# A fourth slot for copied products, the fifth tile's parts in unused quarters of weight tiles, and 2 KB of descriptor room for GpSimd's transfers

## The chip, the core and the metric

The kernel runs on one core of one Trainium2 chip. A time is the device time of one execution in microseconds (us); of several executions of one kernel the median counts. The engines are TensorE (PE; its weight loads PEld), VectorE (DVE), ScalarE (ACT), GpSimd (POOL) and SyncE (SP). Each runs its own list of instructions in order and waits on semaphores for the others. Transfers between HBM and the on-chip memory SBUF, or within SBUF, are issued by SP and POOL and moved by 16 DMA engines that both share. PE writes to PSUM only, in banks of 512 floats a partition.

## The reference

```python
attn_out = softmax(scale * rope(q) @ rope(k).T) @ v      # 2 x 8 heads, 576 rows, 64 columns
x = ((x @ w1) * (x @ w2)) @ w3 @ w_out                   # 1152 x 512, inner width 1024
# third part, on that x:
P = np.exp(logits - logits.max())                        # 1152 x 8, from x @ w_gate
for _ in range(8):
    P /= P.sum(1, keepdims=True) + 1e-09
    P /= P.sum(0, keepdims=True) + 1e-09
    P *= N / E
out = np.zeros((N, D), dtype=np.float32)
for e in range(E):                                       # E = 8 experts
    h = np.maximum(x @ w1[e], 0.0)                       # 512 -> 1024
    ye = h @ w2[e]                                       # 1024 -> 512
    out += P[:, e:e + 1] * ye
```

## The kernel before

The change lies in the third part, the eight experts. Each float32 operand is held as a high and a low part in the fast format, and a product is three matmuls (high by high, high by low, low by high). An expert is cut into two halves of its inner width, so there are 16 **steps** s. A step has two **groups** q = 2s and q = 2s+1 over the rows of x: the first takes 640 rows (columns of 320 on PE), the second 512 (columns of 256). In a group both matrix products, x @ w1 and h @ w2, are done by Strassen's scheme, on 2 x 2 blocks with seven block products in place of eight: A11, A12, A22, S1 to S4 in the code. `hidden(q, u, f)` (L823 to 835) is one product of the first kind, for half u of the inner width; `project(q, f)` (L939 to 961) is one of the second.

Since a PSUM bank must be free for the next product while several products are added into one result, three products of each kind are copied out by ACT: `hidden_copy` (L838) into `tmp`, and `project_copy` (L980) into `ztmp`, which has three slots. The three copies of a group are called zm1 (slot 0), zu2 (slot 1) and **zm7** (slot 2, from bank zQ). `project_sum` (L985, 987) adds a later product to a slot, `weight` (L1004) multiplies the slot by the rows' gate on ACT, and `added` (L1007) lets POOL add the slot to the result `acc` (the tile `sums` in the code) by an accumulating transfer of 256 KB. The three results are called c11, c21 and c22; c22 lies in slot 2. A slot is free for the next group's copy when its transfer has landed.

The 640 rows of a first group are five tiles of 128; Strassen's scheme covers four, and the **fifth tile** goes through plain products: `rest_hi` (L888) and `rest_lo` make high and low parts of it in a tile `HL` (hl in the rows), and `project_rest` (L968 to 970) multiplies them into bank zL, once a step.

Weights for Strassen's scheme need sums of blocks. SP loads blocks into `wide` and `sums` tiles; POOL adds others to them in place by accumulating transfers (`first_accumulate`, `second_accumulate`, all through L899): for each of the two halves of w1 a chain of three (256, 128, 128 KB; sadd in the code), and for w2 a chain of three (512, 256, 256 KB; tadd). `w1hi` (L1131) and `f2hi` (L933) are ACT's copies of the finished sums into high parts. So POOL issues 15 transfers a step: 6 of w1, 3 of w2 and 6 of `acc` (three a group), all in the order of its list.

The order on every engine comes from a planner: each task names its engine, a cost, a rank, what it needs and which slots it takes and frees; `Plan.order` plays that through and lets each engine take the ready task of least rank. POOL's transfers have a cost of KB/146 us on a made-up engine `sw`, with a signal of 1.5 us. The planner sets only the order. What is waited for on the chip is set by the real semaphores.

Of the kernel before, what the change touches and what calls it, by code (L numbers as in the profile page):

```python
# [11 lines left out]
F32 = mybir.dt.float32  # L12
F32R = mybir.dt.float32r
# [6 lines left out]
P = 128  # L20
# [33 lines left out]
class Plan:  # L54
# [2 lines left out]

    SIGNAL = dict(pe=0.28, act=0.14, dve=0.1, pool=0.12, sp=3.0, sw=1.5)  # L60
# [62 lines left out]
def attention_two_moes(ctx: ExitStack, tc: tile.TileContext, rope, qk, v, mw12, mw3t, mwo, wg, ew1, ew2, out):  # L123
# [10 lines left out]
    def f32(ap):  # L134
        return ap.bitcast(F32)
# [650 lines left out]
    pp = ctx.enter_context(tc.tile_pool(name="pp", bufs=1, space=PSUM))  # L786

    tmp = h_p.tile([P, 3, CN[0]], F32, name="tmp")
    ztmp = h_p.tile([P, 3, 2, 256], F32, name="ztmp")
    sums = h_p.tile([P, NTT, DM], F32, name="acc")  # L790
    lgT = sums[: 2 * E].rearrange("p t d -> p (t d)")[:, :NT]
    lg = h_p.tile([P, NTT, E], F32, name="lg")
# [46 lines left out]

    def hidden_sum(q, u, j, b, slot):  # L840
        n = CN[q % 2]
        dst, ps, was = raw[:, j, u, :n], bank[b, q, u][:, :n], tmp[:, slot, :n]
        if j == 0:
            dve.tensor_add(dst, ps, was)  # L844
        elif j == 1:
            dve.tensor_sub(dst, ps, was)
        else:
            negated(dst, ps, ALU.add, was)

    def rectified_last(q, u):  # L850
        n = CN[q % 2]
        act.activation(raw[:, 2, u, :n], bank["T", q, u][:, :n], AF.Relu)  # L852

    def source(f):
        if f in SLOT:
            return raw[:, SLOT[f], :, :256]
        return {S3: held, S4: held, S1: raw[:, 2, :, :256], S2: raw[:, 3, :, :256]}[f]

    def form_sum(f):

        a11, a12, a21, a22 = (raw[:, j, :, :256] for j in range(4))
        if f == S3:
            rectified(held, a11, ALU.subtract, a21)
        elif f == S1:
            rectified(a21, a22, ALU.subtract, a21)
        elif f == S2:
            rectified(a22, a22, ALU.add, held)
        else:
            rectified(held, a12, ALU.subtract, a22)
# [11 lines left out]
        else:  # L881
            dve.tensor_sub(HF[f][:, 1], source(f), f32(HF[f][:, 0]))

    rest = raw[:, :, :, 256 : CN[0]].rearrange("p (b i) u n -> p b (i u) n", b=2)
    restf = [HL[:, x].rearrange("p f (b n) -> p b f n", b=2) for x in range(2)]

    def rest_hi(b):
        act.activation(restf[0][:, b], rest[:, b], AF.Relu)  # L888

    def rest_lo(b):  # L890
        rectified(restf[1][:, b], rest[:, b], ALU.subtract, f32(restf[0][:, b]))

    def sums_tile(src):
        t = h_p.tile([P, 1024], F32, name="sums", bufs=3)
# [81 lines left out]
    def block(q, b, d):  # L976
        return sums[:, out_tiles(q, b), d * 256 : (d + 1) * 256]

    def project_copy(q, b, k):
        act.copy(ztmp[:, k], bank["z" + b, q])  # L980

    def project_sum(q, b, k, out=None):
        dst = ztmp[:, k] if out is None else block(q, *out)
        if b == "T":
            negated(dst, bank["zT", q], ALU.subtract, ztmp[:, k])  # L985
        else:
            dve.tensor_add(dst, bank["z" + b, q], ztmp[:, k])

    def weighted(q, b, d, t, src):
        tt = out_tiles(q, b).start + t  # L990
        acc, p = sums[:, tt, d * 256 : (d + 1) * 256], (npr if src is None else pr)[:, tt, q // 4 : q // 4 + 1]
        ps = bank["zT", q][:, t] if src is None else ztmp[:, src, t]
        dve.scalar_tensor_tensor(out=acc, in0=ps, scalar=p, in1=acc, op0=ALU.mult, op1=ALU.add)

    def weighted_part(q, b, d, t, src, negative):
        tt = out_tiles(q, b).start + t
        acc, p = sums[:, tt, d * 256 : (d + 1) * 256], (npr if negative else pr)[:, tt, q // 4 : q // 4 + 1]
        part = ztmp[:, src, t] if isinstance(src, int) else bank["z" + src, q][:, t]
        dve.scalar_tensor_tensor(out=acc, in0=part, scalar=p, in1=acc, op0=ALU.mult, op1=ALU.add)

    def weight(q, b, src):
        for t in range(2):
            tt = out_tiles(q, b).start + t
            act.activation(ztmp[:, src, t], ztmp[:, src, t], AF.Copy, scale=pr[:, tt, q // 4 : q // 4 + 1])  # L1004

    def added(q, b, d, src):
        pool.dma_start(block(q, b, d), ztmp[:, src], accum_op=ALU.add)  # L1007

    def weighted_rest(q):
        p = pr[:, 4, q // 4 : q // 4 + 1]  # L1010
# [93 lines left out]

# [51 lines left out]
    def hidden_tasks(q):  # L1156

        s, c = divmod(q, 2)
        n, was = CN[c], q - 1
        clear = {  # L1160
            0: [("hi", was, A11), ("lo", was, A11), ("sum", was, S3)],
            1: [("hi", was, A12), ("lo", was, A12), ("sum", was, S4)],
            2: [("hi", was, S1), ("lo", was, S1)],
            3: [("hi", was, S2), ("lo", was, S2), ("sum", was, S4)],
        }
        rests = lambda j: [] if c else old(*((("rest" + y, q - 2, j // 2)) for y in ("hi", "lo")))
        for u in range(2):
            r = 14 * q + 7 * u
            at = {f: r + k for k, f in enumerate(PRODUCTS)}
            h = lambda f: ("h", q, u, f)  # L1170
            a = lambda x: (x, q, u)
            more = {A11: [], S3: [], A12: [], S2: [a("m1")], A22: [a("m7")], S1: [a("u2")], S4: [("r", q, u, 3)]}
            for k, f in enumerate(PRODUCTS):
                weights = [("w1lo", s, u, int(f >= S1))] if s else []
                earlier = [h(PRODUCTS[k - 1])] if k else old(("h", q - 1 + u, 1 - u, S4))
                task(h(f), "pe", 6 * (0.1467, 0.12)[c], at[f], lambda u=u, f=f: hidden(q, u, f), weights + more[f] + earlier, [(HBANK[f], (q, u))] if f in OPENS else [])
            for k, (x, f, b) in enumerate((("m1", A11, "T"), ("u2", S2, "T"), ("m7", S3, "Q"))):
                task(a(x), "act", n - 30, at[f] + 0.2, lambda u=u, b=b, k=k: hidden_copy(q, u, b, k), [h(f)], [(x, (q, u))])
            for k, (j, f, b, y) in enumerate(((0, A12, "A", "m1"), (1, A22, "Q", "u2"), (3, S1, "T", "m7"))):
                needs = [h(f), a(y)] + old(*clear[j]) + rests(j)  # L1180
                task(("r", q, u, j), "dve", n, at[f] + 0.3, lambda u=u, j=j, b=b, k=k: hidden_sum(q, u, j, b, k), needs, (), [(y, (q, u))] + ([] if b == "T" else [(b, (q, u))]))
            needs = [h(S4)] + old(*clear[2]) + rests(2)
            task(("r", q, u, 2), "act", n, at[S4] + 0.3, lambda u=u: rectified_last(q, u), needs, (), [("T", (q, u))])

    def form_tasks(q):
# [19 lines left out]
        ):  # L1205
            task(("sum", q, f), "dve", 512, r + at - lead, lambda f=f: form_sum(f), needs)
        if c == 0:
            for b in range(2):
                task(("resthi", q, b), "act", 256, r + REST_AT - 5, lambda b=b: rest_hi(b), rows(2 * b, 2 * b + 1) + old(("zr", q - 2)))
                task(("restlo", q, b), "dve", 256, r + REST_AT - 5, lambda b=b: rest_lo(b), [("resthi", q, b)])  # L1210
            needs = [("restlo", q, b) for b in range(2)] + [("f2lo", s, ROW0), ("f2lo", s, ROW1)]
# [164 lines left out]
```

## Time and profile before

| | |
|---|---|
| median of 3 runs | 1167.8 us (1160.49 to 1169.78) |
| the profiled execution's own time | 1162.56 us |
| its span in the profile | 1160.8 us |
| mean granted clock of PE, share of full speed | 0.991 |
| PE busy | 1113.1 us (96%) |
| DVE, ACT, POOL busy | 795.2, 666.8, 325.2 us (69, 57, 28%) |
| transfers of POOL's queue | 55.33 MB, 32.2% of 16 engines' span |
| transfers of SP's queue | 109.94 MB, 30.0% |

Some 1.8 us of the execution lie outside the span. The experts' part fills the span from about 370 us to the end; attention and the first layer come before it. Matmuls are pipelined in the record: one of 256 columns is shown with 0.28 us and starts 0.12 us after the one before it, so a busy PE is read by the distance of starts. POOL is shown busy while it issues a transfer, not while the transfer runs.

### The profile page before, as it was taken

The numbers are of one execution on the slowest core, as the hardware profiler recorded it, in microseconds if no ns is written. First come the engines' busy times: TensorE is split into PE (matmuls) and PEld (weight loads), VectorE is DVE, ScalarE is ACT, GpSimd is POOL, SyncE is SP. The second block draws the span as 40 slices with busy tenths as digits, with TensorE's granted clock in tenths as the row PEclk, the third lists the DMA queues.
The fourth block names the chain that finished last, engine by engine and source line by source line (L and its number), as shares of the span: only waits on it lengthen the run. The fifth ranks groups of instructions, "written<-read, shape, count | busy, mean of one in ns | idle before, by whom it ended". The sixth has DMA issues, their size and how long they took to land.

```text
span 1160.8 us, 21261 instructions
## 1 busy us (share of the span) xinstructions
PE 1113.1 (96%) x8233; PEld 1054.2 (91%) x8233; DVE 795.2 (69%) x1391; ACT 666.8 (57%) x1391; POOL 325.2 (28%) x289
## 2 busy tenths in 40 slices
PE   9999999999999999999899999999999899899997
PEld 8887777999998899999899999999999899898997
DVE  7888675744333888767677776875777666586765
ACT  5877775643223556646566565655665546566553
POOL 1665521000000212323333333233333323333220
PEclk9999999999999999999999999999999999999999
DMA  7777733610004646777787887877868677687633
GB/s 237 235 223 205 240 110 110 218 55 1 1 1 121 145 103 164 144 154 162 143 182 149 168 173 140 183 140 165 177 147 167 128 151 161 137 182 142 139 55 103
DMA packets 86308, 167.20 MB, mean 144 GB/s; under 512 B 9536, under 2 KB 50240, under 8 KB 86208
## 3 DMA queue, kind: packets, MB, share of 16 engines
q0 software_dynamic: 47632, 55.33, 32.2%
q1 hardware_dynamic: 38032, 109.94, 30.0%
q8 instruction: 64, 1.05, 0.4%
q10 hardware_dynamic: 544, 0.59, 0.2%
q14 instruction: 36, 0.29, 0.1%
HBM read 112.02 MB, written 2.36 MB: 99 GB/s over the span
## 4 chain that ended last, share of the span: by engine, by line
PE 53%; DMA 10%; ACT 8%; issue 7%; DVE 3%; POOL 1%; ACTq 0%; DVEq 0%; POOLq 0%; SPq 0%
DMA acc<-ztmp 5%; PE T L833 4%; PE T L835 4%; PE T L834 4%; PE zT L959 3%; PE zT L961 3%; PE zT L960 3%; DMA sums<-sums 3%; PE s L153 3%; PE s L154 3%; PE s L155 3%; ACT hf L875 2%; PE Q L833 2%; PE zQ L961 2%; PE zQ L960 2%
## 5 line engine op out<-in xcount | busy, mean ns | idle before, releaser
L1007 POOL DMA_DIRECT2D acc<-ztmp x87 | 108.9, 1251 | 271.3 <-issue 63.6
L899 POOL DMA_DIRECT2D sums<-sums x92 | 94.0, 1024 | 213.0 <-issue 58.4
L959 PE MATMUL zT<-f,hf 128*128 128x256 f32 x496 | 141.0, 284 | 0.0
L961 PE MATMUL zT<-f,hf 128*128 128x256 f32 x496 | 140.4, 283 | 0.1
L960 PE MATMUL zT<-f,hf 128*128 128x256 f32 x496 | 140.4, 283 | 0.0
L899 POOL DMA_DIRECT2D sums<-in_ew_dram x46 | 54.6, 1187 | 216.8 <-DMA sums<-in_ew_dram 167.3
L833 PE MATMUL T<-x,w 128*128 128x320 f32 x256 | 84.0, 328 | 24.5 <-ACT tmp L838 22.0
L980 ACT COPY ztmp<-zQ 128x512 f32<-128x512 f32 x31 | 18.2, 586 | 146.0 <-DMA acc<-ztmp 131.5
L959 PEld LDWEIGHTS zT<-f,hf 128*128 128x128 f32 x496 | 95.1, 192 | 0.7 <-DVE acc L145 0.2
L961 PEld LDWEIGHTS zT<-f,hf 128*128 128x128 f32 x496 | 95.2, 192 | 0.3 <-DVE hf L148 0.3
L960 PEld LDWEIGHTS zT<-f,hf 128*128 128x128 f32 x496 | 95.1, 192 | 0.0
L148 DVE SCALAR_TENSOR_TENSOR y<-y 128x512 f32<-128x512 f32 x128 | 88.0, 688 | 2.4 <-ACT y L852 0.2
L844 DVE TENSOR_TENSOR y<-A,tmp 128x320 f32<-128x320 f32 (+1 forms) x64 | 29.0, 453 | 81.3 <-ACT tmp L838 66.2
L835 PE MATMUL T<-x,w 128*128 128x320 f32 x256 | 79.6, 311 | 0.0
L834 PE MATMUL T<-x,w 128*128 128x320 f32 x256 | 79.4, 310 | 0.0
L875 ACT ACTIVATE hf<-y 128x512 fp32r<-128x512 f32 x128 | 77.6, 629 | 2.9 <-DVE y L148 2.4
L1004 ACT ACTIVATE ztmp<-ztmp,pr 128x256 f32<-128x256 f32 x174 | 78.6, 500 | 0.7 <-DVE ztmp L145 0.3
L148 DVE SCALAR_TENSOR_TENSOR hf<-y,hf 128x512 fp32r<-128x512 f32 x96 | 64.8, 686 | 20.6 <-ACT hf L873 20.5
L153 PE MATMUL s<-x,w 128*128 128x320 f32 (+1 forms) x256 | 76.0, 297 | 0.3 <-DVE gf L678 0.3
L833 PEld LDWEIGHTS T<-x,w 128*128 128x128 f32 x256 | 48.6, 190 | 30.4 <-ACT tmp L838 24.5
L154 PE MATMUL s<-x,w 128*128 128x320 f32 (+1 forms) x256 | 75.8, 296 | 0.0
L155 PE MATMUL s<-x,w 128*128 128x320 f32 (+1 forms) x256 | 75.8, 296 | 0.0
(305 smaller groups left out, 3833.9 us busy)
## 6 DMA issues: line engine op xcount, KB each, us to landing
sums<-in_ew_dram SPq DMA_DIRECT2D x62, 512.0 KB, 4.0
acc<-ztmp POOLq DMA_DIRECT2D x87, 256.0 KB, 4.2
wide<-in_ew_dram SPq DMA_DIRECT2D x34, 512.0 KB, 4.8
wide<-in_ew_dram SPq DMA_DIRECT2D x30, 384.0 KB, 3.6
wide<-in_mw3t_dram SPq DMA_DIRECT2D x16, 512.0 KB, 5.0
wide<-in_mw_dram SPq DMA_DIRECT2D x16, 512.0 KB, 3.3
sums<-in_ew_dram POOLq DMA_DIRECT2D x16, 512.0 KB, 7.0
sums<-sums POOLq DMA_DIRECT2D x32, 256.0 KB, 3.8
```

The source lines that it names most:

```text
L148: dve.scalar_tensor_tensor(out=dst, in0=a, scalar=0.0, in1=b, op0=ALU.max, op1=op)
L153: pe.matmul(ps, wh, xh, start=(i == 0), stop=False)
L154: pe.matmul(ps, wh, xl, start=False, stop=False)
L155: pe.matmul(ps, wl, xh, start=False, stop=(i == n - 1))
L833: pe.matmul(ps, h[:, ws], x[0], start=(first and k == 0), stop=False, **kw)
L834: pe.matmul(ps, h[:, ws], x[1], start=False, stop=False, **kw)
L835: pe.matmul(ps, l[:, ws], x[0], start=False, stop=(k == 1), **kw)
L899: pool.dma_start(dst, src, accum_op=ALU.add)
L959: pe.matmul(ps[:, t], h, wh[:, u], start=(opens and u == 0), stop=False, **kw)
L960: pe.matmul(ps[:, t], h, wl[:, u], start=False, stop=False, **kw)
L961: pe.matmul(ps[:, t], l, wh[:, u], start=False, stop=(u == 1), **kw)
L1007: pool.dma_start(block(q, b, d), ztmp[:, src], accum_op=ALU.add)
```

## The change

Five edits. `ztmp` gets a fourth slot, and the zm7 copy of odd groups goes there (`slot`), so that zm7 copies take slots 2 and 3 in turn; the plan has two places for zm7. The tile `HL` is gone: the fifth tile's parts lie in columns 768 to 1023 of the four plain w1 tiles, which were unused; for that the blocks lie in another order in `raw` (`AT_RAW`), and `rest_hi` and `rest_lo` go over one half u with all four blocks, in place of one row block with both halves. The room for descriptors of POOL's transfers (`dynamic_dma_scratch_size`) goes from 1024 to 2048 bytes a partition. The planner takes POOL's transfers as longer (KB/120 for KB/146, signal 2.0 for 1.5), and two ranks of loads go from 28 to 26 ahead.

```diff
-    SIGNAL = dict(pe=0.28, act=0.14, dve=0.1, pool=0.12, sp=3.0, sw=1.5)
+    SIGNAL = dict(pe=0.28, act=0.14, dve=0.1, pool=0.12, sp=3.0, sw=2.0)
...
-    ztmp = h_p.tile([P, 3, 2, 256], F32, name="ztmp")
+    ztmp = h_p.tile([P, 4, 2, 256], F32, name="ztmp")
...
-    HL = h_p.tile([P, 2, 4, P], F32R, name="hl")
+    AT_RAW = 0, 2, 1, 3
...
-    def rest_hi(b):
-        act.activation(restf[0][:, b], rest[:, b], AF.Relu)
+    def rest_parts(u, x):
+        return W1[u][0][x][:, 768:]
+
+    def rest_views(u, x):
+        return rest_parts(u, x).rearrange("p (m n) -> p m n", m=4), raw[:, :, u, 256 : CN[0]]
+
+    def rest_hi(u):
+        dst, src = rest_views(u, 0)
+        act.activation(dst, src, AF.Relu)
...
+    def slot(q, k):
+        return 3 if k == 2 and q % 2 else k
+
     def project_copy(q, b, k):
-        act.copy(ztmp[:, k], bank["z" + b, q])
+        act.copy(ztmp[:, slot(q, k)], bank["z" + b, q])
...
-    plan = Plan(T=2, A=1, Q=1, zT=1, zQ=1, zA=1, zL=1, wide=2, sums=3, m1=1, u2=1, m7=1, zm1=1, zu2=1, zm7=1)
+    plan = Plan(T=2, A=1, Q=1, zT=1, zQ=1, zA=1, zL=1, wide=2, sums=3, m1=1, u2=1, m7=1, zm1=1, zu2=1, zm7=2)
...
-    AHEAD, AHEAD2 = 28, 28
+    AHEAD, AHEAD2 = 26, 26
...
-        plan.step(name, {"sw": kb / 146}, rank, lambda e: None, [("issue", *name)], (), frees)
+        plan.step(name, {"sw": kb / 120}, rank, lambda e: None, [("issue", *name)], (), frees)
...
-    nc = _bacc.Bacc("TRN2", target_bir_lowering=False, num_devices=1, dynamic_dma_scratch_size=1024)
+    nc = _bacc.Bacc("TRN2", target_bir_lowering=False, num_devices=1, dynamic_dma_scratch_size=2048)
```

PE's order of tasks is the same before and after. POOL's and SP's are the same from the second step on. On ACT some rows change places. From the second group of a middle step, before (hf are the high parts of h, 4239 that of A22, 4242 of S1, 4240 of S2; w_3680 is a w1 tile; DMASW is a lane of POOL's transfers, DMAHW one of SP's):

```order
L838 COPY tmp<-T 128x256 [waits PE_49]
L838 COPY tmp<-Q 128x256 [waits PE_49]
L873 ACTIVATE hf_4239<-y_3959 128x512
L875 ACTIVATE hf_4242<-y_3959 128x512 [waits DVE_49]
L980 COPY ztmp<-zT 128x512 [waits DMASW5_49,PE_49]
L838 COPY tmp<-T 128x256 [waits PE_49]
L1131 CAST w_3680<-wide 128x768 [waits DMAHW6_49,PE_49]
L875 ACTIVATE hf_4240<-y_3959 128x512 [waits DVE_49]
L875 ACTIVATE hf_4241<-y_3959 128x512 [waits DVE_49]
L875 ACTIVATE hf_4243<-y_3959 128x512 [waits DVE_49]
L980 COPY ztmp<-zQ 128x512 [waits DMASW1_49,PE_49]
```

The same place after (L980 is now L988, and L1131 is L1139):

```order
L838 COPY tmp<-T 128x256 [waits PE_49]
L875 ACTIVATE hf_4242<-y_3959 128x512 [waits DVE_49]
L838 COPY tmp<-Q 128x256 [waits PE_49]
L873 ACTIVATE hf_4239<-y_3959 128x512
L988 COPY ztmp<-zT 128x512 [waits DMASW5_49,PE_49]
L838 COPY tmp<-T 128x256 [waits PE_49]
L875 ACTIVATE hf_4240<-y_3959 128x512 [waits DVE_49]
L1139 CAST w_3680<-wide 128x768 [waits DMAHW6_49,PE_49]
L875 ACTIVATE hf_4241<-y_3959 128x512 [waits DVE_49]
L875 ACTIVATE hf_4243<-y_3959 128x512 [waits DVE_49]
L988 COPY ztmp<-zQ 128x512 [waits DMASW2_49,PE_49]
```

The high part of S1 now stands ahead of the copy from Q (m7 in the code), that of S2 ahead of w1hi. The zm7 copy, the last row, still waits for a transfer of POOL, but by its lane and count that is the c22 of two groups before, where it was the c22 of the group before.

Some 30 rows on, in the first group of the next step, before:

```order
L980 COPY ztmp<-zQ 128x512 [waits DMASW1_49,PE_49,Activation_49]
L1004 ACTIVATE ztmp<-ztmp,pr 128x256 [waits DVE_49]
L1004 ACTIVATE ztmp<-ztmp,pr 128x256
L852 ACTIVATE y_3959<-T 128x320 [waits PE_49,Activation_49]
L838 COPY tmp<-T 128x320 [waits PE_49]
L838 COPY tmp<-Q 128x320 [waits PE_49]
L873 ACTIVATE hf_4237<-y_3959 128x512 [waits DVE_49]
```

And after:

```order
L988 COPY ztmp<-zQ 128x512 [waits DMASW1_49,PE_49]
L1012 ACTIVATE ztmp<-ztmp,pr 128x256 [waits DVE_49]
L1012 ACTIVATE ztmp<-ztmp,pr 128x256
L852 ACTIVATE y_3959<-T 128x320 [waits PE_49,Activation_49]
L838 COPY tmp<-T 128x320 [waits PE_49]
L892 ACTIVATE w_3680<-y_3959 128x256 [waits Activation_49]
L838 COPY tmp<-Q 128x320 [waits PE_49]
```

The first of the two rest_hi, now L892 and of half u = 0, comes in between the copies from T and Q; before, it stood some ten rows further down. The lane of the zm7 copy has the same name, but the count waited for is again that of the c22 two groups before.

## Rows read from the trace of the kernel before

**Rows 1.** Timeline of PE: start of project_rest in six steps (start, us, instruction).
```profile
444.65 0.40 PE L968 MATMUL zL<-f,hl 128*128 128x512 f32 x1
...
638.76 0.40 PE L968 MATMUL zL<-f,hl 128*128 128x512 f32 x1
...
684.31 0.40 PE L968 MATMUL zL<-f,hl 128*128 128x512 f32 x1
734.10 0.40 PE L968 MATMUL zL<-f,hl 128*128 128x512 f32 x1
779.64 0.40 PE L968 MATMUL zL<-f,hl 128*128 128x512 f32 x1
829.50 0.40 PE L968 MATMUL zL<-f,hl 128*128 128x512 f32 x1
875.37 0.40 PE L968 MATMUL zL<-f,hl 128*128 128x512 f32 x1
1127.04 0.40 PE L968 MATMUL zL<-f,hl 128*128 128x512 f32 x1
```

**Rows 2.** Windows of one step: busy us (x instructions), PE clock, DMA share, GB/s.
```profile
632.00:677.60 45.60, 45.60 (x351) 44.95 (x350) 34.66 (x56) 29.50 (x60) 14.02 (x14) 1.00 0.81 169
677.60:727.40 49.80, 47.75 (x351) 46.55 (x350) 34.49 (x56) 29.16 (x60) 18.02 (x17) 0.97 0.75 155
```

**Rows 3.** Waits of PE, 440 us to the end: total, times, longest.
```profile
PE T L833 <- ACT tmp L838: 22.0, 12, 3.7
PE Q L833 <- ACT tmp L838: 6.6, 7, 1.8
```

**Rows 4.** Waits of ACT, 440 us to the end.
```profile
ACT ztmp L980 <- DMA acc<-ztmp: 135.7, 26, 8.7
ACT w L1131 <- DMA sums<-sums: 27.5, 9, 4.6
```

**Rows 5.** Timeline of ACT around one zm7 copy; in brackets idle before, releaser.
```profile
697.90 0.90 ACT L1004 ACTIVATE ztmp<-ztmp,pr 128x256 f32<-128x256 f32 x2
...
705.67 1.25 ACT L875 ACTIVATE hf<-y 128x512 fp32r<-128x512 f32 x2
713.77 0.58 ACT L980 COPY ztmp<-zQ 128x512 f32<-128x512 f32 x1 [6.86 <-DMA acc<-ztmp]
```

**Rows 6.** Timeline of PE just behind that copy.
```profile
715.85 0.41 PE L833 MATMUL T<-x,w 128*128 128x320 f32 x1 [1.92 <-ACT tmp L838]
```

**Rows 7.** Window behind that wait; PE clock is the third last number.
```profile
716.70:720.10 3.40, 3.40 (x18) 3.40 (x17) 0.98 (x2) 1.45 (x4) 1.22 (x1) 0.50 0.84 118
```

**Rows 8.** Timeline of POOL: issues of transfers, two places.
```profile
703.93 1.19 POOL L1007 DMA_DIRECT2D acc<-ztmp  x1 [3.12 <-DVE w L1132]
709.58 1.21 POOL L1007 DMA_DIRECT2D acc<-ztmp  x1 [4.46 <-issue]
714.01 1.20 POOL L899 DMA_DIRECT2D sums<-sums  x1 [3.21 <-issue]
...
856.79 1.20 POOL L899 DMA_DIRECT2D sums<-sums  x1 [3.02 <-issue]
857.51 1.40 POOL L899 DMA_DIRECT2D sums<-in_ew_dram  x1
```

**Rows 9.** Chain that ended last: one transfer, from issue to landing.
```profile
709.58 4.09 DMA acc<-ztmp
```

**Rows 10.** The line L899, all transfers of weight sums, issue to landing.
```profile
DMA to landing us min/median/max: 2.6/5.0/9.8
```

**Rows 11.** Page, DMA issues by SP: count, KB each, us to landing.
```profile
wide<-in_ew_dram SPq DMA_DIRECT2D x34, 512.0 KB, 4.8
```

**Rows 12.** Timeline of PE, last group.
```profile
1148.83 0.39 PE L959 MATMUL Q<-f,hf 128*128 128x256 f32 x1 [2.83 <-ACT ztmp L980]
```

**Rows 13.** Timeline of ACT: a copy from Q, and what PE releases next.
```profile
727.10 0.37 ACT L838 COPY tmp<-Q 128x256 f32<-128x256 f32 x1
...
730.58 0.83 ACT L1131 CAST w<-wide 128x768 fp32r<-128x768 f32 x1 [0.23 <-PE Q L834]
```

More of the change, by code (lines that the diff above doesn't have):

```diff
@@ L841, in hidden_sum @@
         n = CN[q % 2]
-        dst, ps, was = raw[:, j, u, :n], bank[b, q, u][:, :n], tmp[:, slot, :n]
+        dst, ps, was = raw[:, AT_RAW[j], u, :n], bank[b, q, u][:, :n], tmp[:, slot, :n]
         if j == 0:
@@ L851, in rectified_last @@
         n = CN[q % 2]
-        act.activation(raw[:, 2, u, :n], bank["T", q, u][:, :n], AF.Relu)
+        act.activation(raw[:, AT_RAW[2], u, :n], bank["T", q, u][:, :n], AF.Relu)
     def source(f):
         if f in SLOT:
-            return raw[:, SLOT[f], :, :256]
-        return {S3: held, S4: held, S1: raw[:, 2, :, :256], S2: raw[:, 3, :, :256]}[f]
+            return raw[:, AT_RAW[SLOT[f]], :, :256]
+        return {S3: held, S4: held, S1: raw[:, AT_RAW[2], :, :256], S2: raw[:, AT_RAW[3], :, :256]}[f]
     def form_sum(f):
-        a11, a12, a21, a22 = (raw[:, j, :, :256] for j in range(4))
+        a11, a12, a21, a22 = (raw[:, j, :, :256] for j in AT_RAW)
         if f == S3:
@@ L882, in form_lo, with rest_lo @@
             dve.tensor_sub(HF[f][:, 1], source(f), f32(HF[f][:, 0]))
-    rest = raw[:, :, :, 256 : CN[0]].rearrange("p (b i) u n -> p b (i u) n", b=2)
-    restf = [HL[:, x].rearrange("p f (b n) -> p b f n", b=2) for x in range(2)]
-    def rest_hi(b):
-        act.activation(restf[0][:, b], rest[:, b], AF.Relu)
-    def rest_lo(b):
-        rectified(restf[1][:, b], rest[:, b], ALU.subtract, f32(restf[0][:, b]))
+    def rest_parts(u, x):
[5 more added lines that the diff above has]
+        act.activation(dst, src, AF.Relu)
+    def rest_lo(u):
+        dst, src = rest_views(u, 1)
+        rectified(dst, src, ALU.subtract, f32(rest_views(u, 0)[0]))
     def sums_tile(src):
@@ L965, in project_rest @@
         for m, (i, u) in enumerate((i, u) for i in range(2) for u in range(2)):
-            h, l = (HL[:, x, 2 * i + u] for x in range(2))
+            h, l = (rest_parts(u, x)[:, i * P : (i + 1) * P] for x in range(2))
             wh, wl = (F2[(ROW0, ROW1)[i]][x][:, u] for x in range(2))
@@ L977, in block @@
         return sums[:, out_tiles(q, b), d * 256 : (d + 1) * 256]
+    def slot(q, k):
+        return 3 if k == 2 and q % 2 else k
     def project_copy(q, b, k):
-        act.copy(ztmp[:, k], bank["z" + b, q])
+        act.copy(ztmp[:, slot(q, k)], bank["z" + b, q])
     def project_sum(q, b, k, out=None):
-        dst = ztmp[:, k] if out is None else block(q, *out)
+        dst = ztmp[:, slot(q, k)] if out is None else block(q, *out)
         if b == "T":
-            negated(dst, bank["zT", q], ALU.subtract, ztmp[:, k])
+            negated(dst, bank["zT", q], ALU.subtract, ztmp[:, slot(q, k)])
         else:
-            dve.tensor_add(dst, bank["z" + b, q], ztmp[:, k])
+            dve.tensor_add(dst, bank["z" + b, q], ztmp[:, slot(q, k)])
     def weighted(q, b, d, t, src):
@@ L991, in weighted @@
         acc, p = sums[:, tt, d * 256 : (d + 1) * 256], (npr if src is None else pr)[:, tt, q // 4 : q // 4 + 1]
-        ps = bank["zT", q][:, t] if src is None else ztmp[:, src, t]
+        ps = bank["zT", q][:, t] if src is None else ztmp[:, slot(q, src), t]
         dve.scalar_tensor_tensor(out=acc, in0=ps, scalar=p, in1=acc, op0=ALU.mult, op1=ALU.add)
@@ L997, in weighted_part @@
         acc, p = sums[:, tt, d * 256 : (d + 1) * 256], (npr if negative else pr)[:, tt, q // 4 : q // 4 + 1]
-        part = ztmp[:, src, t] if isinstance(src, int) else bank["z" + src, q][:, t]
+        part = ztmp[:, slot(q, src), t] if isinstance(src, int) else bank["z" + src, q][:, t]
         dve.scalar_tensor_tensor(out=acc, in0=part, scalar=p, in1=acc, op0=ALU.mult, op1=ALU.add)
@@ L1003, in weight @@
             tt = out_tiles(q, b).start + t
-            act.activation(ztmp[:, src, t], ztmp[:, src, t], AF.Copy, scale=pr[:, tt, q // 4 : q // 4 + 1])
+            act.activation(ztmp[:, slot(q, src), t], ztmp[:, slot(q, src), t], AF.Copy, scale=pr[:, tt, q // 4 : q // 4 + 1])
     def added(q, b, d, src):
-        pool.dma_start(block(q, b, d), ztmp[:, src], accum_op=ALU.add)
+        pool.dma_start(block(q, b, d), ztmp[:, slot(q, src)], accum_op=ALU.add)
     def weighted_rest(q):
@@ L1165, in hidden_tasks @@
         }
-        rests = lambda j: [] if c else old(*((("rest" + y, q - 2, j // 2)) for y in ("hi", "lo")))
+        rests = lambda u: [] if c else old(*((("rest" + y, q - 2, u)) for y in ("hi", "lo")))
         for u in range(2):
@@ L1179, in hidden_tasks @@
             for k, (j, f, b, y) in enumerate(((0, A12, "A", "m1"), (1, A22, "Q", "u2"), (3, S1, "T", "m7"))):
-                needs = [h(f), a(y)] + old(*clear[j]) + rests(j)
+                needs = [h(f), a(y)] + old(*clear[j]) + rests(u)
                 task(("r", q, u, j), "dve", n, at[f] + 0.3, lambda u=u, j=j, b=b, k=k: hidden_sum(q, u, j, b, k), needs, (), [(y, (q, u))] + ([] if b == "T" else [(b, (q, u))]))
-            needs = [h(S4)] + old(*clear[2]) + rests(2)
+            needs = [h(S4)] + old(*clear[2]) + rests(u)
             task(("r", q, u, 2), "act", n, at[S4] + 0.3, lambda u=u: rectified_last(q, u), needs, (), [("T", (q, u))])
@@ L1207, in form_tasks @@
         if c == 0:
[L1208 to L1211, printed above, removed]
+            for u in range(2):
+                rows_u = [("r", q, u, j) for j in range(4)]
+                task(("resthi", q, u), "act", 256, r + REST_AT - 5, lambda u=u: rest_hi(u), rows_u + old(("zr", q - 2)))
+                task(("restlo", q, u), "dve", 256, r + REST_AT - 5, lambda u=u: rest_lo(u), [("resthi", q, u)])
+            needs = [("restlo", q, u) for u in range(2)] + [("f2lo", s, ROW0), ("f2lo", s, ROW1)]
             task(("zr", q), "pe", 12 * 0.2267, r + REST_AT + 0.6, lambda: project_rest(q), needs, [("zL", q)])
```

## Prediction

> **What bounds the kernel now.** I read the page first: PE is busy for 1113.1 of 1160.8 us, and no other engine reaches 70%. So the time is PE's, and the question is where PE stands still. Since a busy PE is not one at its peak, I measured steps, by the start of the fifth tile's product, which stands at one fixed place in every step [rows 1]. The 14 steps from 444.65 to 1127.04 take 682.39 us, 48.74 each. They are of two kinds: 638.76 to 684.31 is 45.55, 734.10 to 779.64 is 45.54, 829.50 to 875.37 is 45.87, and those between them are 49.79 and 49.86. The windows show the difference [rows 2]: in the short step PE has no idle time at all (45.60 of 45.60), in the long one 2.05 us, and there the clock is 0.97 and not 1.00. PE does the same work in both, so about 45.65, the mean of the three, is a step in which PE is never kept waiting.
>
> What keeps it waiting is in the waits of PE [rows 3]: 22.0 us in 12 waits at the first matmul of a product into bank T, for an ACT copy that frees it, and 6.6 us in 7 at bank Q. ACT is not busy then. Its own waits say why [rows 4]: 135.7 us in 26 waits of L980 for a transfer `acc<-ztmp` to land, and 27.5 us in 9 of L1131 for `sums<-sums`. One such place, by time: ACT is done with the h parts at 706.92, stands for 6.86 us, copies zm7 at 713.77 [rows 5], and the hidden copies behind it in its list come late, so that PE starts its product at 715.85 after 1.92 us idle [rows 6]. Then the clock falls: 0.50 of full speed from 716.70 to 720.10, the lower level of 1.2 GHz, right behind an idle PE [rows 7]. At half speed those 3.4 us are worth 1.7, so this wait cost nearly 4 us, about all that a long step has over a short one.
>
> The transfer that ACT waits for was issued at 709.58 and took 4.09 us [rows 9]. Its data had been ready at 698.80, when `weight` ended [rows 5]: it stood 10.8 us in POOL's queue. POOL itself was not working: each issue takes 1.2 us, and before it POOL stands for 3 to 4.5 us [rows 8]. The rows name causes like "issue" that explain nothing, but the times do. The transfer of 709.58 lands at 713.67, and POOL starts the next at 714.01, 0.34 us later, although that one adds two other tiles. A transfer of sums and one from HBM can go out 0.72 us apart (856.79 and 857.51), two of `acc<-ztmp` nowhere do. So POOL most likely waits for the room for descriptors that the diff names, and the whole queue of 15 transfers a step is passed nearly one by one. **The resource that sets the pace is that queue, seen through ACT and then PE.**
>
> **The change, part by part.** *The fourth slot.* The zm7 copy waits for the c22 transfer of two groups before. That one is older by a group, some 24 us (half of 48.74), and the wait to be covered was 6.86 and at most 8.7, so it has landed. All 26 waits [rows 4] lie at this copy: 135.7 us of ACT, of which PE feels 22.0 and the clock that falls behind them. Behind the wait stood the hidden copies, so PE's waits at T go with it.
>
> *Descriptor room doubled.* Two large transfers and two small ones can be under way where it was one and one. The next issue then comes 1.2 us after the last [rows 8], not when it has landed, some 3 us earlier for each large one. The c22 of rows 5, two or three places back in the queue when its data were ready, leaves some 6 to 9 us earlier. That would nearly remove the zm7 wait by itself (6.86), so the two edits cover for each other there. Alone it also moves up the weight chains: L1131's 27.5 us are waits for the third transfer of a chain whose first was held up behind c21 and c22; the longest, 4.6, is less than what the queue gives back. PE's 6.6 us at bank Q follow L1131 and go with them.
>
> *The fifth tile's parts.* As many instructions, of the same size. Moved: the first rest_hi comes between the copies from T and Q. An ACT copy of 128x256 takes 0.37 us, so the copy from Q is that much later; it ended at 727.47, and PE's product in Q released an ACT instruction only at 730.58 [rows 13], so some 3 us lie between: nothing, covered by the products in between; without the cover 0.4 us a step, 6 in all. The high part of S1 ahead of that copy, likewise. No row of the new order shows an added wait at w1hi or at the fifth tile's product, which now share a tile.
>
> *The planner's numbers* change no cost on the chip; POOL's and SP's orders differ only before the second step, which I put at nothing.
>
> *The sum.* All steps at 45.65 in place of 48.74: 14 x 3.09 = 43.3 us. In the last group PE waits 2.83 us for the same copy [rows 12], in another slot after the change: 2.8. Together 46.1. The steps before 444.65 never wait for these transfers and stay. Not all of it will come: the three short steps differ by 0.3, the moved copies may show by 0.4, and other small waits step forward when the large ones go. I keep back 0.5 a step, 7 us. So 39.1 us less: 1162.56 - 39.1 = **1123 us**. The profiled execution is 5 us under the median of the three; I add nothing for that, since what differs between executions is most likely how long these same waits are.
>
> What is late next is PE itself, at 12 matmuls a product without a gap.
>
> **The rivals.** *(A) The room changes nothing* (POOL waits for something else, or the argument doesn't reach it). Then only the slot acts, and the queue's pace stays. In rows 1 a long and a short step take 47.7 on average, which is the fastest that the queue went through two steps; at that pace 14 x 1.07 = 15 us and 2.8 are gained, at the present one 2.8. That is 1145 to 1160, say 1150. For it: every wait of POOL has some name in the rows; against it: the 0.34 us behind a landing.
>
> *(B) More transfers under way only take longer each.* A step needs 0.81 x 45.6 = 36.9 us of the 16 engines by one row and 0.75 x 49.8 = 37.4 by the other [rows 2], so at 45.65 they would be 82% busy: what the short steps bore. But weight sums already take up to 9.8 us where the median is 5.0 [rows 10]; a chain of three at twice the median is 14 us longer, more than the 10.8 of queueing that it loses. If 2 us a step are left of that for PE, 28 us of the 46 are lost: 1144. The Trainium skill has a rule that speaks for it: "DMA: Bandwidth & Descriptors", section "Issuing engines are not separate DMA queues", says that transfers from all issuers run on the same 16 engines and interleave, so that issuing more at once saves only the issuer's time. By that rule alone the transfers would land no sooner, and the room would give what (A) gives. The trace agrees that the engines are shared, but not that they are full: 0.75 in a long step.
>
> *(C) Slower:* the weights' own loads on SP are held up by POOL's transfers, which now crowd the engines. A load of 512 KB takes 4.8 us [rows 11]. It decides from the point where PE waits more than 46.1/14 = 3.3 us a step for w1hi or f2hi; with a doubled load wholly bare, 4.8 a step, the time is 1162.56 + 14 x 4.8 - 46.1 = 1184. Against it: from 440 us on, no wait of ACT names such a load.
>
> **How the numbers follow.** Forecast 0.80, (A) 0.08, (B) 0.09, (C) 0.03. Lowest: all 46.1 and a little from the steps before 444.65, 1113. Upwards the range takes in (B) and ends short of (A): 1113 to 1144. A measurement of this kernel tells 1% from no change, at 1156 and 1179 us. The forecast, (B) and most of (A) are faster than 1156; (A)'s upper part is within 1%; (C) is slower: 0.93, 0.04, 0.03.
>
> **What would show it.** Right: L980 has no wait for `acc<-ztmp`; two issues of `acc<-ztmp` stand 1.2 us apart with no landing between; the steps of rows 1 are all 45.6 to 46.3; PE has no window at clock 0.97 after 444. If the steps alternate between 45.6 and 47 or more and POOL still starts 0.3 us behind landings, it is (A). If landings in rows 10 go to 7 us or more and ACT's L1131 waits for `sums<-sums` longer than 27.5, it is (B). If ACT waits for `wide` loads, (C). I would be wrong as a whole if PE idles elsewhere as soon as ACT is free, above all if short steps were short because PE had waited the step before.

## The result and the profile after

The change takes the kernel to 1111.1 us (median of 4 runs, 1110.08 to 1112.66), against 1165.49 (4 runs, 1160.49 to 1169.78) for the kernel before: a ratio of 0.9536, with a 95% interval of 0.9492 to 0.958. The forecast was 1123, with 1113 as the lowest, so the time lies 1.9 us below the range. The profiled execution took 1112.66 us with a span of 1110.9.

The page of the profile answers first: PE is now busy for nearly the whole span. A transfer of `acc` takes 5.6 us in the median, where it took 4.2 before, and the wide loads take less than the 4.8 us of [rows 11]. The last line is that of the kernel before:

```profile
PE 1096.0 (99%) x8233; PEld 1043.9 (94%) x8233; DVE 797.4 (72%) x1391; ACT 672.2 (61%) x1391; POOL 323.1 (29%) x289
...
acc<-ztmp POOLq DMA_DIRECT2D x87, 256.0 KB, 5.6
wide<-in_ew_dram SPq DMA_DIRECT2D x34, 512.0 KB, 4.1
...
acc<-ztmp POOLq DMA_DIRECT2D x87, 256.0 KB, 4.2
```

The timeline of PE has the marks of [rows 1], the start of project_rest, now in line 973: the first, a pair in the middle, the one behind it, and the last.

```profile
445.33 0.40 PE L973 MATMUL zL<-f,w 128*128 128x512 f32 x1
...
672.60 0.40 PE L973 MATMUL zL<-f,w 128*128 128x512 f32 x1
718.05 0.40 PE L973 MATMUL zL<-f,w 128*128 128x512 f32 x1
...
1081.69 0.40 PE L973 MATMUL zL<-f,w 128*128 128x512 f32 x1
```

14 steps take 636.36 us, 45.45 each, where they took 48.74. All are of one length. The windows of two steps in a row show PE without a gap and at the full clock. Behind them stand the end behind the last mark, where the clock falls only in the last microseconds, and that end in the kernel before:

```profile
672.60:718.00 45.40, 45.40 (x350) 44.81 (x349) 34.70 (x56) 29.74 (x58) 15.84 (x15) 1.00 0.80 167
718.10:763.50 45.40, 45.40 (x349) 44.81 (x349) 34.69 (x56) 29.72 (x58) 15.87 (x15) 1.00 0.83 173
...
1081.69:1110.90 29.21, 24.72 (x194) 23.87 (x192) 19.13 (x38) 11.31 (x23) 3.60 (x3) 0.99 0.43 109
...
1127.04:1160.80 33.76, 26.45 (x194) 25.39 (x192) 19.59 (x38) 11.22 (x23) 3.60 (x3) 0.94 0.37 94
```

So the 49.9 us between the two spans (1160.8 and 1110.9) lie in three stretches. Up to the first mark: 0.7 more. The 14 steps: 682.39 - 636.36 = 46.0 less. Behind the last mark: 33.8 before (1160.8 - 1127.04), 29.2 now, 4.6 less.

From 440 us on, PE has no wait of the kind in [rows 3] left at all. None of ACT's waits there names a transfer any more; the longest are waits for PE and DVE, which cost nothing as long as PE has its data.

```profile
ACT ztmp L988 <- PE zQ L966: 51.7, 29, 2.1
ACT ztmp L988 <- PE zT L966: 45.5, 57, 1.1
...
ACT hf L873 <- DVE y L844: 23.2, 28, 1.0
ACT w L1139 <- PE Q L834: 18.7, 15, 1.3
```

POOL's timeline at one c22 (687.16; the two issues ahead of it are one of sums and c21) and ACT's around it:

```profile
683.86 1.20 POOL L904 DMA_DIRECT2D sums<-sums  x1 [5.81 <-DVE y L846]
685.23 1.19 POOL L1015 DMA_DIRECT2D acc<-ztmp  x1 [0.17 <-issue]
687.16 1.21 POOL L1015 DMA_DIRECT2D acc<-ztmp  x1 [0.74 <-ACT tmp L838]
689.98 1.20 POOL L904 DMA_DIRECT2D sums<-sums  x1 [1.60 <-DMA sums<-sums]
```

```profile
685.90 0.89 ACT L1012 ACTIVATE ztmp<-ztmp,pr 128x256 f32<-128x256 f32 x2
...
696.66 0.59 ACT L988 COPY ztmp<-zQ 128x512 f32<-128x512 f32 x1 [2.06 <-PE zQ L966]
```

Three transfers of 256 KB (683.86, 685.23, 687.16) go out within 3.3 us, less than the 5.6 us that one takes to land. The weights of c22 end at 685.90 + 0.89 = 686.79, and it is issued 0.37 us later; in [rows 5, 8] it was 10.8. The next zm7 copy at 696.66 waits for PE, as it should.

### The profile page after: what moved, and what is told of

Same layout as the page of the kernel before. It is cut to its first block, busy times and chain, and to the rows that moved or that the text cites. A ratio compares the mean times of both kernels' runs of the same rounds, so it can differ in the third digit from the quotient of the medians.

```text
span 1110.9 us, 21233 instructions
## 1 busy us (share of the span) xinstructions
PE 1096.0 (99%) x8233; PEld 1043.9 (94%) x8233; DVE 797.4 (72%) x1391; ACT 672.2 (61%) x1391; POOL 323.1 (29%) x289
## 4 chain that ended last, share of the span: by engine, by line
PE 75%; DMA 4%; DVE 1%; ACT 1%; issue 0%; DVEq 0%; ACTq 0%; POOLq 0%; SPq 0%
PE T L833 6%; PE T L834 6%; PE T L835 6%; PE zT L964 5%; PE zT L966 5%; PE zT L965 5%; PE s L153 3%; PE s L154 3%; PE s L155 3%; PE Q L833 3%; PE Q L834 3%; PE Q L835 3%; PE zQ L966 3%; PE zQ L965 3%; PE zQ L964 3%; DMA wide<-in_mw_dram 2%
## 5 line engine op out<-in xcount | busy, mean ns | idle before, releaser
L964 PE MATMUL zT<-f,hf 128*128 128x256 f32 x496 | 141.0, 284 | 0.0
L904 POOL DMA_DIRECT2D sums<-in_ew_dram x46 | 41.8, 909 | 277.5 <-DMA sums<-in_ew_dram 167.1
L964 PEld LDWEIGHTS zT<-f,hf 128*128 128x128 f32 x496 | 94.9, 191 | 0.6 <-DVE acc L145 0.2
L833 PE MATMUL T<-x,w 128*128 128x320 f32 x256 | 81.1, 317 | 0.0
L875 ACT ACTIVATE hf<-y 128x512 fp32r<-128x512 f32 x128 | 78.4, 632 | 1.6 <-DVE y L148 1.4
L835 PE MATMUL T<-x,w 128*128 128x320 f32 x256 | 79.2, 309 | 0.0
L834 PE MATMUL T<-x,w 128*128 128x320 f32 x256 | 79.2, 309 | 0.0
L873 ACT ACTIVATE hf<-y 128x512 fp32r<-128x512 f32 x96 | 60.0, 627 | 28.7 <-DVE y L844 24.4
L833 PE MATMUL T<-y,w 128*128 128x256 f32 x256 | 72.9, 285 | 2.1 <-ACT tmp L838 1.6
L835 PE MATMUL T<-y,w 128*128 128x256 f32 x256 | 72.5, 283 | 0.0
```

The lines of the kernel that those rows point to most:

```text
L833: pe.matmul(ps, h[:, ws], x[0], start=(first and k == 0), stop=False, **kw)
L834: pe.matmul(ps, h[:, ws], x[1], start=False, stop=False, **kw)
L835: pe.matmul(ps, l[:, ws], x[0], start=False, stop=(k == 1), **kw)
L904: pool.dma_start(dst, src, accum_op=ALU.add)
L964: pe.matmul(ps[:, t], h, wh[:, u], start=(opens and u == 0), stop=False, **kw)
```

## The experiments

The theory ahead of them took up the prediction's cause, that POOL's queue waits for room for descriptors, and went further than it: the room alone brings the gain, and the slot is covered by it. The first rival gives the gain to the slot (a wait for one slot removed), the second to the order (fifth tile, planner's numbers). Four kernels take the change apart; then the room is varied, and last the place of the data in SBUF, which became a question on the way. Ratios are to the kernel before, run on the same chip.

**e1, the fifth tile's parts alone.** Three slots, 1024 bytes, the planner's old numbers. Against the changed kernel:

```diff
-    ztmp = h_p.tile([P, 4, 2, 256], F32, name="ztmp")
+    ztmp = h_p.tile([P, 3, 2, 256], F32, name="ztmp")
-        return 3 if k == 2 and q % 2 else k
+        return k
-    plan = Plan(..., zm7=2)      # sw, AHEAD and kb / 146 too as in the kernel before
+    plan = Plan(..., zm7=1)
-    nc = _bacc.Bacc(..., dynamic_dma_scratch_size=2048)
+    nc = _bacc.Bacc(..., dynamic_dma_scratch_size=1024)
```

> Of the change only the fifth tile's parts in the w1 tiles (and the blocks' order in raw); three slots, 1024 bytes of room and the planner's numbers as before. Theory R (the room for descriptors sets the pace of POOL's queue): as before, 1160 to 1170 us, steps long and short in turn, L980's successor waits some 130 us for acc transfers. A rival M (moved instructions, the shared tile or SBUF's layout play a part of their own): more than 5 us away from the kernel before, either way.

1170.1 us, a ratio of 1.0004 (0.997 to 1.0038). The waits of ACT from 440 us on are those of [rows 4]:

```profile
ACT ztmp L988 <- DMA acc<-ztmp: 146.2, 25, 8.9
...
ACT w L1139 <- DMA sums<-sums: 22.2, 7, 4.6
```

This part gives and costs nothing that can be measured. The next ones are built on it.

**e2, the room alone.** e1 with 2048 bytes:

```diff
-    nc = _bacc.Bacc(..., dynamic_dma_scratch_size=1024)
+    nc = _bacc.Bacc(..., dynamic_dma_scratch_size=2048)
```

> The first kernel and 2048 bytes of room; three slots and the planner's numbers as before. Theory R: nearly the whole gain. In the changed kernel the c22 transfer landed 1.6 to 5 us before the next group's zm7 copy began (-1.5 in the last group), so the third slot would have been free in time: 1111 to 1116 us, steps at 45.45 to 45.8, ACT's waits for acc transfers under 10 us in all. Theory S (the fourth slot takes the wait away, the room is an aside): 1150 us or more, since the copy still waits for the group before. Theory B (more transfers under way only take longer each): zm7 still waits 2 us or more a group, 1130 us or more.

1114.58 us, 0.9509 (0.9456 to 0.9562). With three slots and the old numbers, ACT waits for no transfer from 440 us on, and all that is left of PE's waits there is one in the last group, where 2.83 us were [rows 12]:

```profile
PE Q L964 <- ACT ztmp L988: 0.7, 1, 0.7
```

The steps take 45.46 us (448.33 to 1084.73). The room by itself brings nearly the whole gain. It also moves tiles in SBUF by 1024 bytes, which matters further down, but that is not the gain here: the shortest of e1's steps, from 1095.11 to 1140.57, is as long as those of e2.

**e3, the slot alone.** The changed kernel, its order and its four slots, with 1024 bytes:

```diff
-    nc = _bacc.Bacc(..., dynamic_dma_scratch_size=2048)
+    nc = _bacc.Bacc(..., dynamic_dma_scratch_size=1024)
```

> The changed kernel with 1024 bytes of room: four slots, the fifth tile's parts in the w1 tiles and the new planner's numbers stay. Theory R: the copy waits no more, but POOL's queue goes at its old pace, so the wait moves to the weight sums (ACT's L1139 for sums<-sums over 40 us in all, 27.5 before) : 1135 to 1160 us, POOL still starts 0.3 us behind a landing. Theory S: 1111 to 1120 us.

1164.09 us, 0.9937 (0.9908 to 0.9966): some 7 us by the ratio, the planner's new numbers included, where the room brings 57. That is 4 us over the range expected. The wait at the zm7 copy is gone, and the waits of ACT and PE from 440 us on show where the time went instead:

```profile
ACT f L938 <- DMA sums<-sums: 46.5, 14, 5.7
...
ACT w L1139 <- DMA sums<-sums: 28.2, 9, 3.9
```

```profile
PE T L833 <- DVE y L145: 29.3, 22, 4.3
PE Q L833 <- ACT tmp L838: 4.3, 6, 1.0
```

I had expected it at w1hi; it came mostly at f2hi, line 938. PE loses no less at bank T than in [rows 3] (29.3 against 22.0). POOL's timeline says why:

```profile
712.39 1.19 POOL L1015 DMA_DIRECT2D acc<-ztmp  x1 [3.03 <-DVE y L844]
716.53 1.21 POOL L1015 DMA_DIRECT2D acc<-ztmp  x1 [2.95 <-issue]
720.90 1.20 POOL L904 DMA_DIRECT2D sums<-sums  x1 [3.15 <-issue]
```

These three transfers of 256 KB still go out 4.1 to 4.4 us apart: the first two land at 716.21 and 720.56, and the next one starts 0.32 and 0.34 us later. The queue keeps its pace, ACT no longer waits for its end at one place, and so waits for it at another.

**e4, the change with the planner's old numbers.**

```diff
-    SIGNAL = dict(..., sw=2.0)
+    SIGNAL = dict(..., sw=1.5)
-    AHEAD, AHEAD2 = 26, 26
+    AHEAD, AHEAD2 = 28, 28
-        plan.step(name, {"sw": kb / 120}, ...)
+        plan.step(name, {"sw": kb / 146}, ...)
```

> The changed kernel with the planner's numbers of before (transfers at KB/146 and 1.5 us, loads 28 ahead). Both theories: no difference from the changed kernel, 1110 to 1113 us, since PE's order doesn't depend on them and PE has no gap left; steps at 45.45. If the numbers matter (an order in which a transfer's result is read too early), steps over 45.6 and 1115 us or more.

1113.04 us, 0.9497 (0.9452 to 0.9541). The steps are 45.45, as in the changed kernel. Since e2 has 0.9509 on the same chip, a fourth slot on top of the room is worth 1.5 us by the medians, which the intervals do not tell from nothing; 0.7 us of it is the wait in the last group.

**e8, the change with the old ranks alone.**

```diff
-    AHEAD, AHEAD2 = 26, 26
+    AHEAD, AHEAD2 = 28, 28
```

> The changed kernel with the loads' ranks 28 ahead as before, the transfers' costs new. The old numbers together gave 1113.0 for 1111.1, with the clock at half speed once near 411 us. If the ranks do that: 1113 and the fall is there. If the transfers' costs do it: 1111 and no fall before the end.

1112.53 us, 0.9521 (0.9462 to 0.9581). The steps are 45.45. Only the first step (the one up to the mark at 445) differs: 50.21 in its profile for 48.69, with a stretch at a lower clock at 412 us, which e4 has too (50.05). The kernel's executions by themselves range from 1109.7 to 1115.14, so those 1.4 us are not settled.

**e5, e6, e7, the room varied.** e1 with 1088, 832 and 768 bytes, one line each:

```diff
-    nc = _bacc.Bacc(..., dynamic_dma_scratch_size=1024)
+    nc = _bacc.Bacc(..., dynamic_dma_scratch_size=1088)   # e5; 832 in e6; 768 in e7
```

> The kernel of e1 with 1088 bytes of room in place of 1024: 68 entries if one takes 16 bytes. Count theory: a transfer in two pieces a partition (acc, or sums of 256 KB) takes 33 entries, one in a single piece 17, and an issue waits until its own fit; then two large ones (66) go out together with 64 bytes more, and most of the gain is there: 1113 to 1130 us, two acc issues 1.2 us apart. Rival, room by bytes or by number of transfers: 6% more room changes little, 1160 to 1172 us.

> The kernel of e1 with 832 bytes: 52 entries. Count theory: one large and one small (33 + 17 = 50) still fit, as with 1024, where two large (66) don't: no change from e1, 1163 to 1176 us. Rival, less room is slower in proportion: 19% less should cost 10 us or more, over 1180.

> The kernel of e1 with 768 bytes: 48 entries. Count theory: one large and one small (50) no longer fit together, two small (34) do: every such pair goes one after the other, some four a step at 3 to 4 us each: over 1200 us, a clear edge between 832 and 768. Rival, in proportion: a few us slower than with 832.

| room, bytes | 768 (e7) | 832 (e6) | 1024 (e1) | 1088 (e5) | 2048 (e2) |
|---|---|---|---|---|---|
| us | 1367.63 | 1163.15 | 1170.1 | 1099.7 | 1114.58 |
| ratio | 1.1698 (1.1617 to 1.178) | 0.9955 (0.9924 to 0.9986) | 1.0004 (0.997 to 1.0038) | 0.9418 (0.9371 to 0.9466) | 0.9509 (0.9456 to 0.9562) |

The time goes in stairs, not in a slope: 64 bytes more than 1024 bring all of the gain, 192 fewer lose nothing, and 256 fewer cost 17%. (That 832 and 1088 bytes come out some us lower still than their neighbours has another cause, told below.) At 768 POOL sends even a large and a small transfer one after the other. Its timeline there, and the waits of ACT and of PE from 440 us on:

```profile
855.15 1.21 POOL L904 DMA_DIRECT2D sums<-sums  x1 [4.56 <-issue]
859.23 0.90 POOL L904 DMA_DIRECT2D sums<-in_ew_dram  x1 [2.86 <-issue]
864.00 1.22 POOL L1015 DMA_DIRECT2D acc<-ztmp  x1 [3.87 <-DVE y L145]
868.90 0.92 POOL L904 DMA_DIRECT2D sums<-sums  x1 [3.69 <-issue]
```

```profile
ACT ztmp L988 <- DMA acc<-ztmp: 271.3, 27, 14.5
```

```profile
PE T L833 <- ACT tmp L838: 122.1, 27, 8.9
```

The transfer of sums and the one from HBM, which went out 0.72 us apart at 1024 [rows 8], stand 4.1 us apart here. At 832 it is the pattern of before, with 139.0 us of waiting at the zm7 copy. At 1088 two of 256 KB within SBUF follow each other at 1.84 us:

```profile
684.01 1.20 POOL L1015 DMA_DIRECT2D acc<-ztmp  x1 [2.27 <-ACT hf L875]
685.85 1.21 POOL L904 DMA_DIRECT2D sums<-sums  x1 [0.64 <-issue]
```

What counts is the number of pieces and not the KB. By the shapes in the traces, `acc` and the w2 sums within SBUF move two pieces of 1 KB a partition; call these large. All others move one piece, of 1, 2 or 4 KB; call these small. One from HBM, of 2 KB a piece, has 256 KB as well, and is still one of the small ones. POOL issues 225 transfers in each run. Counted from their issues and landings, this is what was under way together when one went out (the new one included):

| room, bytes | 768 | 832 | 1024 (e1) | 1088 | 2048 (e2) |
|---|---|---|---|---|---|
| one alone | 193 | 83 | 83 | 39 | 41 |
| two small | 32 | 31 | 31 | 18 | 18 |
| one large, one small | 0 | 111 | 111 | 84 | 72 |
| one large, two small | 0 | 0 | 0 | 27 | 24 |
| two large | 0 | 0 | 0 | 57 | 30 |
| two large and one more | 0 | 0 | 0 | 0 | 40 |

So two large ones fit into 1088 bytes and not into 1024, which makes 512 to 544 for one; a large one and a small one fit into 832 and not into 768, which makes some 224 to 320 for the small one (832 - 512 is the most, 768 - 544 the least). The Trainium skill, "DMA: Bandwidth & Descriptors", section "Terms", says that a descriptor is a struct of 16 bytes and that those for GpSimd's transfers are written to rings in SBUF. By that, and this is an estimate, 1024 bytes hold 64, and 33 for a large transfer and 17 for a small one would fit all four edges (33 + 33 = 66 and 33 + 17 = 50, against 68, 64, 52 and 48). The runs agree with the edges, and one large with two small (67) goes out at 1088 and never at 1024; no row counts the descriptors.

e5 held a surprise: 1099.7 us is 14.9 less than with 2048. The steps are 44.62 long (443.74 to 1068.35), not 45.45, with PE without a gap in both. The groups of L964 from 440 us on show it in the matmul itself, of the changed kernel and then of e5:

```profile
L964 PE MATMUL zT<-f,hf 128*128 128x256 f32 x461 | 131.0, 284 | 0.0
```

```profile
L964 PE MATMUL zT<-f,hf 128*128 128x256 f32 x460 | 128.1, 279 | 0.0
```

In the traces only the matmuls of 256 columns differ. Counted over twelve steps, with distances above 0.2 us left out, they start 120.2 ns (zT, zQ) and 119.9 ns (T, A, Q) apart in the changed kernel, 117.0 and 116.4 in e5. Those of 320 columns start 146.8 and 146.6 ns apart, those of 512 columns some 229 in both.

Between 2048 and 1088 bytes, the tiles behind the descriptors lie 960 bytes lower, which is 64 off a multiple of 128. Two theories: the place of the data sets it, or something in the smaller room does. The next four tell them apart.

**e9, e11, e12, an unused tile ahead of all others.** The changed kernel, its 2048 bytes kept, with a tile of 64, 128 or 32 bytes a partition ahead of those on the left side of SBUF, which so start higher by that much. The parts of w1 and w2 and the load tiles are there; what kernel.py allocates with `side="right"` (the parts of x and h, `ztmp`, `acc`) is not:

```diff
+    pad = base.tile([P, 16], F32, name="pad")     # e9; 32 columns in e11; 8 in e12
+    nc.gpsimd.memset(pad, 0.0)
```

**e10, the whole change with 1088 bytes.**

```diff
-    nc = _bacc.Bacc(..., dynamic_dma_scratch_size=2048)
+    nc = _bacc.Bacc(..., dynamic_dma_scratch_size=1088)
```

> The changed kernel, room 2048 as it is, with an unused tile of 64 bytes a partition ahead of all others, so that the tiles on the left side of SBUF (w1 and w2 parts among them) start 64 bytes higher, as they do with 1088 bytes of room. In e5 a step took 44.60 us where the changed kernel takes 45.45, with no gap on PE in either: matmuls of 256 columns start 117 ns apart and not 120. Theory P (where the operands start in SBUF sets the pace of matmuls): steps of 44.6 us, 1097 to 1100 us. Rival Q (the smaller room does it, fewer transfers under way, less traffic): 45.45, 1110 to 1113 us.

> The changed kernel with 1088 bytes of room in place of 2048: e5 with the fourth slot and the new numbers. Both theories: steps at 44.6, and what the slot and the numbers still give, 0.7 us in the last group and 1 to 2 in the first step: 1096 to 1099 us, the fastest of all. If the slot makes POOL's smaller queue lag: over 1100.

> As e9 with 128 bytes. Theory P with a period of 128 bytes (the changed kernel's first w1 tile starts at byte 11232, 96 over a multiple of 128, that of e5 at 10272, 32 over one): the same remainder as the changed kernel, 45.45 and 1110 to 1113 us. Any shift helps: 44.6.

> As e9 with 32 bytes: w1 tiles start at a multiple of 128. Theory P with aligned operands as the best case: 44.6 or less, at most 1100 us. If the remainder 32 is what is good, or 64 bytes apart from the others: 45.45, 1110 to 1113 us.

| | shift, bytes | us | ratio | a step, us |
|---|---|---|---|---|
| after | 0 | 1111.1 | 0.9536 (0.9492 to 0.958) | 45.45 |
| e12 | +32 | 1104.04 | 0.946 (0.9397 to 0.9524) | 44.86 |
| e9 | +64 | 1102.61 | 0.9437 (0.938 to 0.9494) | 44.64 |
| e11 | +128 | 1109.72 | 0.9509 (0.9457 to 0.9561) | 45.19 |
| e10 | -960 | 1099.88 | 0.9422 (0.937 to 0.9474) | 44.65 |

The steps are the marks of project_rest divided by 14; in e9, for one:

```profile
447.34 0.40 PE L975 MATMUL zL<-f,w 128*128 128x512 f32 x1
...
1072.36 0.40 PE L975 MATMUL zL<-f,w 128*128 128x512 f32 x1
```

It is the place: e9 has the room of the change and the steps of e5. The size of the room has no part in it: at 832 bytes, another shift of 64 off a multiple of 128, matmuls of 256 columns start 117.1 and 116.6 ns apart as well, and at 768, 1024 and 2048 bytes 120. So the times at 832 and 1088 above hold a gain from the place too, for 1088 some 12 us: 14 steps of 45.46 in e2, of 44.62 in e5.

That the pattern repeats every 128 bytes, as I had supposed for e11, does not hold to the digit: 45.19 is neither 45.45 nor 44.64. Nor is e12 better than e9, as one theory had it. The steps are the measure here. The times of e9, e10 and e12 came out 1 to 4 us above what was expected, and those of e9, e11 and e12 hold falls of the clock in the first step (told in the last section), each worth 1.7 us, that the changed kernel's profile and e10's do not have. What was moved are the parts of w1, the first operand of `pe.matmul` in `hidden`, and those of w2, the second one in `project`; both kinds of product became faster. Why, stays open. e10 and e5 are the fastest versions, 1099.88 and 1099.7 us, and beat both kernels; with the room there, no gain of four slots over three can be measured.

## Where the prediction was right, and the step that failed

The mechanism was right. PE was the bound, and POOL's queue, seen through ACT, held it up: with the queue's pace alone changed (e2) the gain is there, and with the pace worsened alone (e7) PE loses 122.1 us at the very bank of [rows 3]. In the trace of the kernel before, PE is idle for 31.2 us in the 14 steps, and the clock falls to half speed four times for 3.4 us, worth 6.8; in the changed kernel both are nothing. The other 8.0 of the 46.0 us stand in no idle time. They lie around the 32 gaps, by an estimate from the starts of matmuls: the one ahead of a gap is shown as busy beyond the usual distance of starts (0.28 us for 0.12), 5.1 us in all, and the first six behind it are further apart than usual, 3.3 us in all.

*The 7 us kept back* are the step that failed: "I keep back 0.5 a step". Nothing of it came. No small wait of PE stepped forward, the moved copies showed nowhere, and every step is as long as the next.

*The sum of 46.1 us* was too small as well. 43.3 for the steps and 2.8 for the end were forecast; measured were 46.0 and 4.6, and 0.7 the other way up to the first mark. The steps came to 45.45, not 45.65: I had taken the mean of three short steps, one of which was 45.87, and not the shortest, 45.54. That is 14 x 0.2 = 2.8. At the end I counted the 2.83 us of idle PE and not the clock behind it; the window behind the last mark had 0.94 and has 0.99 now, and 4.6 us came. I had counted exactly that for the steps [rows 7].

With 7.0 + 2.7 + 1.8 - 0.7 = 10.8, that is the whole distance between 1162.56 - 39.1 and the profiled 1112.66; the median lies 1.6 lower, as the profiled execution is the slowest of the four. The range's lower end, 1113, was the sum with nothing kept back, 1116.5, and 3.5 more for the steps before 444.65, where nothing was gained; the two terms that came out larger took 4.5.

*"They are of two kinds"* holds for the steps shown in [rows 1] and not for all. Only those three of the 14 are near 45.5; the others take 47.2 to 52.6 us, and only four of them have a fall of the clock. The sum did not need it, since it goes by the mean of all 14, but rival (A) did: 47.7 is not the fastest that the queue went through two steps. Those from 590.76 to 684.31 take 46.8 each, and at that pace (A) would have reached down to some 1132, inside the range. Nor did the whole queue pass nearly one by one: 142 of the 225 transfers went out beside one other (its counts are those of e1 in the table above). It is the large ones that never went out beside each other.

*"The two edits cover for each other"* was half right. The room covers for the slot (e2, e5 against e10); the slot does not cover for the room (e3). "Behind the wait stood the hidden copies, so PE's waits at T go with it" failed: with the slot alone the wait at the copy is gone, and 29.3 us at T are there. The text had the reason, that a slot leaves the queue's pace as it is, and used it in rival (A).

*Rival (A)*, that the room changes nothing, is refuted by e2. Its price for the slot, 2.8 to 18 us, holds the 7 of e3, in part by luck, as its upper end was worked out from too few steps.

*Rival (B)*, that more transfers under way only take longer, is half true: `acc` took 4.2 us in the median and takes 5.6. The weight sums do not take longer. In the changed kernel, the lines of added and of the weight sums show these times from issue to landing (in [rows 10] the latter was 2.6/5.0/9.8):

```profile
DMA to landing us min/median/max: 3.7/5.6/7.9
...
DMA to landing us min/median/max: 2.6/4.9/8.2
```

So a transfer of `acc` gets slower by 1.4 us; but c22 leaves some 10 us sooner, and even the chains of sums, where each waits for the one ahead, end in time. The slower landings agree with the Trainium skill, "DMA: Bandwidth & Descriptors", section "Issuing engines are not separate DMA queues", that the engines are shared. That section speaks of issuing from several engines at once, which saves only the issuer's time; here one engine issues more at once. The issuer's time is what was saved here too, and it was not small: POOL stood until a landing, 3 to 4.5 us a time [rows 8], and that was what the kernel waited for.

*Rival (C)* did not come: wide loads went from 4.8 to 4.1 us.

*The rest* was rightly put at nothing: the fifth tile (e1) and the planner's numbers (e4, e8).

## What to carry to other kernels

When an engine that issues transfers stands idle, look at what its next issue follows: if that is the landing of an unrelated transfer, some 0.3 us before, whatever cause the row names, its transfers most likely wait for room, and the few bytes that are missing can be worth some 5%, as the 64 here. Varying the room in small amounts shows it. A wait that is removed at one place while the queue behind it keeps its pace comes back at the next place that reads from the queue. When a trace already has steps without any wait, the shortest of them is the forecast, and what is kept back for the unknown belongs into the range, not into the time.

## What was not expected of the hardware

With PE never waiting and at the full clock, the same matmuls took 45.45, 45.19, 44.86 or 44.64 us a step, by where the tiles of the left side of SBUF start (0, 128, 32 or 64 bytes higher). Only the matmuls of 256 columns change: they start 120 ns apart in the slowest layout and 117 in that of e5. Between e2 and e5 that is 1.8% of a step and 11.8 of the 14.9 us between the two kernels, more than any edit of the change but the room (the slot alone: some 7). No run here tells the reason.

The second thing is the clock in the first step: in e4 and e8, at some 411 us, it falls to the lower level of 1.2 GHz for 3.4 us, and that step takes 50.05 and 50.21 us; the changed kernel has no such fall in its profile, and 48.69. The profiles of the kernel before and of e1, e2, e6, e11 and e12 have the fall as well, at 409 to 414 us, that of e3 has one at 392, that of e9 one at 393 and one at 413; e5, e7 and e10 have none. It is not the ranks that decide: e11 and e12 have those of the changed kernel, and e5 has the old ones. Nor is it the idle time of PE just before, which is alike with the fall and without: 0.95 and 0.54 us at 409 to 411 us in the changed kernel, 0.95 and 0.54 us at 408 to 410 in e8. What decides it was not found.
